# A tilted list schedule, z on VectorE alone, V shifted by DMA, and q and k in pieces

## The chip, the cores and the metric

One core of one Trainium2 chip. The metric is the device time of one execution in microseconds; less is better. Before: 210.66 us, the median of 3 runs (210.21 to 212.92). A profiled execution has a span (first to last instruction) some 2 us shorter than its time; the one of before took 208.38 us, 2.3 less than the median. On one core a run is called slow when it lies over 1.5% above the fastest run of the same kernel; fast runs are compared with fast runs. The kernel before was run beside every experiment on the same chip, and the ratios below are against those runs.

## The reference, cut to what matters

```python
# attention: 4 batches, 8 heads, 768 positions, 64 per head
scores = q @ k.T / 8                      # causal; heads 0, 2, 6 see all of it ("retrieval"),
                                          # heads 1, 3, 4, 5, 7 a window of 64 and 4 sink rows ("streaming")
x = softmax(scores) @ v                   # heads side by side: 768 x 512
# token mix
theta = x @ w_theta
y = w_tok_r @ (x * cos(theta)) + w_tok_i @ (x * sin(theta))   # "zr" and "zi"
u = x + y
out = u + relu(u @ w_ch)
```

## The kernel before, the parts that matter

The kernel is a list of steps, each with its possible engines and a duration. A list scheduler in the kernel's own program orders them by rank (the longest way to the end), and each engine then runs its steps in that fixed order. The order is static: on the chip an engine whose next step is not ready waits, even if later ones are.

```python
# a step may name two engines; the scheduler picks one
zs[b, "r", i + y] = add("DVE", 690, z_real, [c] + old, give=[c], port=True)
zs[b, "i", i + y] = add({"DVE": 690, "POOL": 1250}, 0, z_imag, [s] + old, give=[s], port=True)
...
cast[b, n] = add({"DVE": 570, "POOL": 830}, 0, cast_v, [land] + old, give=[issue], port=True)   # V to bf16
shift[b, h] = add({"DVE": 340, "POOL": 960}, 0, shift_v, [cast[b, n]] + old, port=True)         # V by 64 rows, streaming heads
...
def load_steps(b, after):                 # q and k of a batch: one transfer each, from GpSimd's queue
    for what in "qk":
        issue = add("POOL", 900, lambda: load_qk(what, b, slice(0, 8)), after + last_pool, bias=-20000)
        land = add("DMA", 5000, None, [issue])
...
first = add("SP", 1500, lambda: sink_values(2 * half), ...)     # sink rows of V for two batches
land = add("DMAH", 300, None, [first])
sink_done.append(add("DVE", 480, <cast of them into vs>, [land, ...]))
...
order = plan.order({"PE": 0, "ACT": 2100, "DVE": 2500, "POOL": 7500, "SP": 750})
for s in order:                           # emitted in the order of planned start
    ...
```

The softmax here doesn't subtract the row's maximum and nothing guards it: scores larger than these inputs give would overflow.

## Time and profile before

TensorE has 179.0 us of work in a span of 206.3. The prediction below cuts the span into windows and shows in which of them TensorE stands idle. In the profile's lines PE is TensorE and PEld its weight loads, DVE is VectorE, ACT ScalarE, POOL GpSimd and SP SyncE; a q behind the name (SPq) means the engine's queue. The two groups that carry z are shown here (line, engine, operation, shapes and count, then busy us, mean ns of one, then idle time before them and what ended it):

```profile
L243 POOL TENSOR_TENSOR zi<-x,st 128x512 bf16<-128x512 bf16 x11 | 14.7, 1350 | 29.0 <-ACT st L486 28.9
L243 DVE TENSOR_TENSOR zr<-x,ct 128x512 bf16<-128x512 bf16 x24 | 22.9, 992 | 1.5 <-ACT ct L484 1.5
```

GpSimd does 11 of the 24 zi; VectorE's zr take 992 ns in the mean beside them.

### The profile page before, as it was taken

To read this page: it belongs to the slowest core of one execution; us is meant where nothing else is said; L and a number is where in the kernel's file an instruction comes from. 1 tells how busy PE (TensorE), PEld (TensorE's weight loads), DVE (VectorE), ACT (ScalarE), POOL (GpSimd) and SP (SyncE) were. 2 spreads that over 40 slices of the span, in tenths; PEclk is the share of its full clock that TensorE was granted. 3 is DMA by queue.
4 is the path that set the end of the run, shared out by engine and by line. 5 is a ranking of instruction groups with operands and counts; after the bars stand their busy time and mean duration, and the time that the engine had idled before them with its cause. 6 is when DMAs were issued, how large, how long until landed. Compare 5 with 4: busy or idle time off the path is not lost.

```text
span 206.3 us, 4846 instructions
## 1 busy us (share of the span) xinstructions
PE 179.0 (87%) x1988; PEld 99.4 (48%) x1988; DVE 134.2 (65%) x236; ACT 108.7 (53%) x135; POOL 76.1 (37%) x140
## 2 busy tenths in 40 slices
PE   0689599667999999999999999989699999597992
PEld 0436388444546584454653557534335664242440
DVE  7336966389984574799855287499917446944442
ACT  2397914789885735550677464696683427300010
POOL 8966960394752000674123200099350002900000
PEclk9999999999999999999999999999999999999999
DMA  5998999999999995952223047784223254113404
GB/s 169 182 222 168 157 199 196 192 202 208 206 204 204 115 126 134 232 144 102 54 81 126 4 78 130 185 180 96 49 81 102 79 102 105 55 47 76 153 25 152
DMA packets 58252, 27.45 MB, mean 133 GB/s; under 512 B 44408, under 2 KB 55160, under 8 KB 58232
## 3 DMA queue, kind: packets, MB, share of 16 engines
q1 hardware_dynamic: 47704, 17.85, 40.6%
q0 software_dynamic: 10528, 9.31, 28.3%
q8 instruction: 15, 0.25, 0.6%
q14 instruction: 5, 0.04, 0.1%
HBM read 25.71 MB, written 6.29 MB: 155 GB/s over the span
## 4 chain that ended last, share of the span: by engine, by line
PE 64%; DVE 14%; DMA 13%; ACT 4%; POOL 2%; issue 1%; DVEq 0%; POOLq 0%
PE bank L502 28%; PE bank L525 9%; DMA qb<-in_q_dram 8%; PE pair L366 7%; DVE zr L243 7%; PE pair L453 7%; PE pair L479 6%; PE bank L300 5%; DMA kb<-in_k_dram 3%; DVE zi L243 2%; DVE qT L240 1%; DMA uT<-u 1%; DVE vx L240 1%; PE bank L545 1%; DMA out_dram<-ot 1%
## 5 line engine op out<-in xcount | busy, mean ns | idle before, releaser
L502 PE MATMUL bank<-zr,wtokTr 128*128 128x512 bf16 x144 | 38.6, 380 | 4.3 <-DVE zr L243 3.4
L502 PE MATMUL bank<-zi,wtokTi 128*128 128x512 bf16 x144 | 38.3, 379 | 0.2 <-DVE zi L243 0.2
L366 PE MATMUL pair<-qT,kT 64*64 64x128 bf16 (+5 forms) x380 | 26.7, 262 | 5.1 <-ACT P L385 2.1
L506 DVE TENSOR_TENSOR u<-x,bank 128x512 bf16<-128x512 bf16 x24 | 16.3, 684 | 18.6 <-PE bank L502 18.5
L525 PE MATMUL bank<-w_ch_sb,uT 128*128 128x512 bf16 x96 | 24.1, 380 | 1.9 <-DMA uT<-u 1.5
L247 POOL TENSOR_SCALAR_AFFINE_SELECT P<-P 128x256 bf16<-128x256 bf16 (+1 forms) x48 | 18.2, 398 | 20.1 <-ACT P L385 11.0
L243 POOL TENSOR_TENSOR zi<-x,st 128x512 bf16<-128x512 bf16 x11 | 14.7, 1350 | 29.0 <-ACT st L486 28.9
L529 DVE SCALAR_TENSOR_TENSOR ot<-bank,u 128x512 f32<-128x512 f32 x24 | 16.5, 689 | 13.5 <-PE bank L525 13.2
L243 DVE TENSOR_TENSOR zr<-x,ct 128x512 bf16<-128x512 bf16 x24 | 22.9, 992 | 1.5 <-ACT ct L484 1.5
L366 PEld LDWEIGHTS <-kT 64*64 64x64 bf16 (+1 forms) x380 | 13.0, 111 | 22.4 <-issue 19.5
L385 ACT ACTIVATE P<-pair 128x1024 bf16<-128x1024 f32 (+2 forms) x24 | 21.8, 922 | 3.0 <-PE pair L366 2.8
L479 PE MATMUL pair<-w_theta_sb,xT 128*128 128x512 bf16 x96 | 22.8, 379 | 0.3 <-ACT st L486 0.2
L502 PEld LDWEIGHTS <-wtokTi 128*128 128x128 bf16 x144 | 13.5, 98 | 17.3 <-issue 2.1
L502 PEld LDWEIGHTS <-wtokTr 128*128 128x128 bf16 x144 | 12.6, 98 | 18.9 <-issue 6.5
L382 ACT ACTIVATE P_st<-pair 128x512 bf16<-128x512 f32 (+1 forms) x16 | 12.8, 813 | 12.9 <-PE pair L366 12.8
L240 ACT COPY uT<-bank 128x512 bf16<-128x512 bf16 x5 | 2.9, 585 | 29.3 <-PE bank L515 29.3
L240 POOL CAST vt<-st_v 128x768 bf16<-128x768 f32 x9 | 10.3, 1167 | 20.7 <-DMA st_v<-in_v_dram 20.6
L484 ACT ACTIVATE ct<-pair,half_pi 128x1024 f32<-128x1024 f32 x12 | 13.1, 1118 | 8.0 <-PE pair L479 5.1
L460 DVE TENSOR_TENSOR x<-pair,r 128x512 bf16<-128x512 f32 x24 | 16.6, 691 | 0.8
L453 PE MATMUL pair<-vx,P_st 128*128 128x65 bf16 x120 | 16.0, 200 | 0.3 <-DVE P_st L402 0.3
L300 PE MATMUL bank<-ident,kb 128*64 128x128 bf16 x192 | 8.9, 244 | 8.4 <-DVE kb L240 5.2
L453 PE MATMUL pair<-vt,P_st 128*128 128x65 bf16 x120 | 16.0, 200 | 0.0
(77 smaller groups left out, 291.6 us busy)
## 6 DMA issues: line engine op xcount, KB each, us to landing
st_v<-in_v_dram SPq DMA_DIRECT2D x32, 192.0 KB
out_dram<-ot SPq DMA_DIRECT2D x24, 256.0 KB
qb<-in_q_dram POOLq DMA_DIRECT2D x3, 768.0 KB, 16.8
kb<-in_k_dram POOLq DMA_DIRECT2D x3, 768.0 KB, 19.6
wtok<-in_moe_w_tok_r_dram POOLq DMA_DIRECT2D x3, 384.0 KB, 15.4
wtok<-in_moe_w_tok_i_dram POOLq DMA_DIRECT2D x3, 384.0 KB, 16.6
w_theta_sb<-in_moe_w_theta_dram POOLq DMA_DIRECT2D x1, 512.0 KB, 9.5
w_ch_sb<-in_moe_w_ch_dram POOLq DMA_DIRECT2D x1, 512.0 KB, 24.3
```

The lines of the kernel that those rows point to most:

```text
L240: {"ACT": nc.scalar.copy, "DVE": nc.vector.tensor_copy, "POOL": nc.gpsimd.tensor_copy}[state["step"].eng](o, i)
L243: {"DVE": nc.vector, "POOL": nc.gpsimd}[state["step"].eng].tensor_tensor(o, a, b, ALU.mult)
L247: nc.gpsimd.affine_select(out=t, in_=t, compare_op=ALU.is_ge, fill=0.0, base=base, pattern=pattern, channel_multiplier=cm)
L300: nc.tensor.transpose(pt[64 * x:64 * x + 64, j * 128:(j + 1) * 128], state[what, b][:, h, j * D:(j + 1) * D], ident)
L366: nc.tensor.matmul(ps[half, yy, c:c + w], l, r, start=True, stop=True, skip_group_check=True)
L385: nc.scalar.activation(P.rearrange("p (y c) -> p y c", y=2), ps[:, :, :w0], AF.Exp, scale=scale)
L453: nc.tensor.matmul(o, l, r, start=(m == 0), stop=True, skip_group_check=True)
L460: nc.vector.tensor_tensor(dst, av[:, :, :, :D], r.unsqueeze(3).to_broadcast([128, 2, 4, D]), ALU.mult)
L479: nc.tensor.matmul(ps[:, y], state["xT", b][:, kk, (i + y) * 128:(i + y + 1) * 128], w_theta_sb[:, kk], start=(kk == 0), stop=(kk == KD - 1))
L502: nc.tensor.matmul(py, wtokT[n][:, s, t * 128:(t + 1) * 128], z[:, s], start=(g == 0 and m == 0), stop=(g == 2 and m == 3))
L525: nc.tensor.matmul(pc, uT[:, kk], w_ch_sb[:, kk], start=(kk == 0), stop=(kk == KD - 1))
L529: nc.vector.scalar_tensor_tensor(ot, state.pop(("pc", b, t)), 0.0, state.pop(("u", b, t)), ALU.max, ALU.add)
```

## The change

Its intent: a table of 800-odd numbers, found by a search against the schedule's own model of durations, is added to the ranks; some durations of that model are corrected; VectorE and GpSimd are no longer planned to work at the same time on operations that want their common port; all of z goes to VectorE; V of batches 1 to 3 is shifted by DMAs from SyncE (SP); q and k of batches 1 to 3 come two heads at a time, and those of batches 2 and 3 are held back until the token mix two batches earlier runs.

```diff
+TILT = [
+    -82, 155, -168, 19, 0, 0, 358, 0, 91, 190, 0, 406, 514, 399, -109, -295, 17, -173, 57, -465, -136, -201, -239,
+    ...                                    (cut: 42 more rows)
+]
+        self.tilt = {n: 100 * t for n, t in enumerate(TILT)}
...
+        for n, ns in self.tilt.items():
+            rank[n] += ns
...
+                other = {"DVE": "POOL", "POOL": "DVE"}.get(e)
+                busy = other and port[other] and free[other] > now
                 for s in ready[e]:
+                    if busy and s.port:
+                        continue
...
+    def move_v(b):
+        for s, h in ((slice(0, 1), slice(4, 5)), (slice(1, 5), slice(1, 8, 2))):
+            nc.sync.dma_start(out=vx[:64, s], in_=vt[:64, h])
+            nc.sync.dma_start(out=vx[64:, s, 1:], in_=vt[64:, h, :NB - 1])
...
-                if not IS_RETR[h]:
-                    shift[b, h] = add({"DVE": 340, "POOL": 960}, 0, ... shift_v ..., [cast[b, n]] + old, port=True)
+                if not IS_RETR[h] and b == 0:
+                    shift[b, h] = add({"DVE": 510, "POOL": 1000}, 0, ... shift_v ..., [cast[b, n]], port=True)
+        if b:
+            move = add("SP", 1400, lambda b=b: move_v(b), [cast[b, n] for n in (1, 2, 3)] + old)
+            moved = add("DMAH", 500, None, [move])
...
-                zs[b, "i", i + y] = add({"DVE": 690, "POOL": 1250}, 0, ... z_imag ..., [s] + old, give=[s], port=True)
+                zs[b, "i", i + y] = add("DVE", 690, ... z_imag ..., [s] + old, give=[s], port=True)
...
+            if t < 4 and b + 2 < B:
+                load_steps(b + 2, t, [kept[what, b, n] for what in "qk" for n in range(4)] + [mixed[b, t, 2]])
...
-    def load_steps(b, after):
+    def load_steps(b, n, after):
+        heads = slice(PAIRS[n][0], PAIRS[n][1] + 1, 2)
         for what in "qk":
-            issue = add("POOL", 900, ... load_qk(what, b, slice(0, 8)) ...)
+            issue = add("POOL", 750, ... load_qk(what, b, heads) ...)
-    load_steps(1, [])
+    for n in range(4):
+        load_steps(1, n, [])
(cut: durations, such as normalize 850 -> 920 and waves 930 -> 1000, one term of the rank formula, and helper lines)
```

## The prediction

> **What bounds the kernel now.** I read the page's busy times first, then the table of windows, the list of waits, and last the timeline of each stall, engine by engine. The busy times:
>
> ```profile
> span 206.3 us, 4846 instructions
> PE 179.0 (87%) x1988; PEld 99.4 (48%) x1988; DVE 134.2 (65%) x236; ACT 108.7 (53%) x135; POOL 76.1 (37%) x140
> ```
>
> TensorE is the bound: 179.0 of 206.3 us, so at most 27.3 us can be won by filling its holes. No part of the change removes a matmul. The windows (window: length, then busy time of PE, weight load, DVE, ACT, POOL, then clock, DMA share, GB/s) say where the holes are:
>
> ```profile
> 0.00:8.84 8.84, 1.65 (x24) 1.22 (x24) 5.07 (x12) 2.88 (x3) 7.55 (x18) 1.00 0.85 172
> 8.84:31.40 22.56, 18.82 (x257) 13.38 (x258) 14.36 (x32) 14.97 (x21) 16.25 (x39) 1.00 1.02 188
> 31.40:57.40 26.00, 20.51 (x312) 13.48 (x310) 20.34 (x36) 20.05 (x26) 13.50 (x20) 1.00 1.24 200
> 57.40:131.00 73.60, 73.60 (x845) 39.98 (x845) 48.50 (x89) 40.40 (x51) 17.89 (x36) 1.00 0.71 122
> 131.00:150.00 19.00, 16.36 (x173) 8.22 (x172) 17.55 (x25) 14.66 (x19) 12.19 (x17) 1.00 0.56 130
> 150.00:172.60 22.60, 22.60 (x267) 11.93 (x265) 10.14 (x21) 10.70 (x14) 2.88 (x8) 1.00 0.39 93
> 172.60:189.00 16.40, 12.41 (x57) 5.33 (x56) 11.67 (x14) 4.43 (x5) 5.87 (x4) 1.00 0.22 67
> 189.00:206.30 17.30, 13.02 (x66) 5.87 (x64) 6.55 (x10) 0.58 (x1) 0.00 (x0) 0.98 0.32 106
> ```
>
> The PE idles 7.2 us before the first data, 3.7 to 31.4 us, 5.5 to 57.4 us, nothing in the long middle, 2.6 at 131 to 150 us, 4.0 at 172.6 to 189 us, and 4.3 in the last window, the tail of last finishes and stores. Start and tail (11.5 us) are touched by nothing here. That leaves 15.8 us to be won.
>
> The second fact is the collision of DVE and POOL over z. In the timeline (start, length, engine, line, instruction, idle before) of the last batch's z:
>
> ```profile
> 173.39 0.68 DVE L243 TENSOR_TENSOR zr<-x,ct 128x512 bf16<-128x512 bf16 x1
> 174.59 4.43 DVE L243 TENSOR_TENSOR zr<-x,ct 128x512 bf16<-128x512 bf16 x3
> 174.17 5.87 POOL L243 TENSOR_TENSOR zi<-x,st 128x512 bf16<-128x512 bf16 x4 [19.71 <-ACT st L486]
> 179.07 2.53 PE L502 MATMUL bank<-zr,wtokTr 128*128 128x512 bf16 x11 [1.19 <-DVE zr L243]
> ```
>
> Three zr take 4.43 us beside POOL's zi, 1.48 each against 0.68 alone; the PE waits for them. The third is the start of batch 1, where all of q and k comes in one transfer each:
>
> ```profile
> 41.36 0.86 PE L300 MATMUL bank<-ident,qb 128*64 128x128 bf16 x24 [1.71 <-DMA qb<-in_q_dram]
> 43.01 0.86 PE L300 MATMUL bank<-ident,qb 128*64 128x128 bf16 x24 [0.79 <-DVE qT L240]
> 46.82 1.20 PE L300 MATMUL bank<-ident,kb 128*64 128x128 bf16 x36 [0.89 <-DMA kb<-in_k_dram]
> 50.11 1.02 PE L502 MATMUL bank<-zr,wtokTr 128*128 128x512 bf16 x4 [0.86 <-DVE kT L240]
> ```
>
> **What the Trainium skill says.** "SBUF — State Buffer", section "SBUF: two separate sides": the port pair that VectorE and GpSimd share is an exclusive lock for a whole instruction, taken also by a VectorE operation with two SBUF inputs against a GpSimd operation that reads SBUF. The trace agrees: zr has a median of 688 ns, a mean of 992 and a maximum of 2168. "DMA: Bandwidth & Descriptors", section "SWDGE vs HWDGE vs iDMA": transfers issued from SyncE do not use GpSimd's descriptor path, so the shift of V cannot be locked out by VectorE. The same page, section "Anatomy of one DMA", puts some 2 us of fixed cost on each transfer of the GpSimd path. Nothing in this trace isolates that: the large q and k loads took 16 to 20 us under a saturated DMA. "TensorE: Matmul & The Clock Gate", Part 1: the array runs at half rate until it has been busy for some 3.4 us. The trace agrees in kind: 24 transposes took 1.49 us at 16.8 us and 0.86 at 41.4, and the fast pace begins only at 31.4 us, though the page's clock row shows full clock throughout.
>
> **The change part by part.**
>
> z on VectorE. 11 products of 1350 ns leave POOL (14.7 us). They add 11 x 0.68 = 7.5 us to DVE, but the stretch goes: zr 22.9 - 24 x 0.69 = 6.3 and zi 11.9 - 13 x 0.69 = 2.9. So DVE is no busier (-1.7), and throughput gains nothing. In the last batch, from 173.39, twelve products and three finishes at the 0.60 us start-to-start of undisturbed ones are 9.0 us, to 182.4; with POOL's help the last one ended at 182.39, the same. What changes is the order: the first mixing group wants four zr only. Alone on DVE they can be ready at 173.4 + 4 x 0.60 = 175.8, or 177.0 behind two finishes, against 179.0. The PE waited 1.30 + 1.19 = 2.5 us there; I take 2.0. Likewise 0.7 at 137 to 139 us, and 0.8 of the wait for kT at 50 us, a copy that stood on DVE behind three stretched zr (4.02 us). Sum 3.5.
>
> q and k in pieces. For batch 1 only the first pair of heads has to land before its transposes, a quarter of each transfer. The waits at 41 to 47 us are 1.71 + 0.79 + 0.89 = 3.4 us. The DMA stays saturated (share 1.24) so the bytes needed come no sooner in sum; I take 2.5. Batches 2 and 3 used to load at 41.8 to 53 us, into that saturated stretch; now they wait for the token mix, where the DMA share is 0.7 or less. This relieves the token weights and costs nothing as long as they land before about 98 and 122 us. POOL issues grow from 6 to 24, 18 x 0.75 = 13.5 us, about what z gives back.
>
> V shifted by DMA. 15 of 20 streaming heads lose two copies of some 0.25 us each: 7.6 us of mostly DVE work. One block of it (2.62 us at 142.4) stands before the u additions, but PE's next wait is for exponentials, not for these. SP gets 12 transfers of some 0.4 to 0.5 us each. V was cast by 146 and is first multiplied at 156, so a landing some us later hides. On the path: 0.3.
>
> The tilted priorities. They aim at what is left of the 15.8: 1.7 at 146 to 150 (PE waits for exponentials that it fed too late), 1.5 at 186.8 (a wait for the transpose of u), and 3.7 before 31.4. That is 6.9; being a static order tuned for a model of durations, I give it 40%, 2.7. The chain also has 24 groups of four large matmuls that take 0.97 instead of 0.86 us because they alternate with the score matmuls' tile shape; this 2.6 us may shrink or grow by some 1 us and is not counted.
>
> Sum: 3.5 + 2.5 + 0.3 + 2.7 = 9.0 us of gain. Off that I take 1.5 for new collisions: POOL issues before causal masks, SP blocked on a V shift ahead of the transposes of x, and order that the chip does not follow as modelled. Net 7.5: 210.7 - 7.5 = 203.2.
>
> **The rivals.** (a) VectorE becomes the bound around each theta stage. For it: DVE is busy 17.55 of 19.0 us at 131 to 150, and all 12 products of a batch are now its own. Against it: without the stretch and the V shift its total falls to about 134.2 - 1.7 - 7.6 = 125 us. It would leave the z gain at zero or below: 207 us. (b) The gain is all in the schedule and larger: PE has 15.8 us of holes, and if an earlier dense start makes the array fast before 31.4 us, some of the 18.8 busy us before it halve. Against it: to 57 us the DMA is saturated, so earlier speed mostly buys more waiting. It would make 198 us. (c) The tilt was tuned on wrong durations and the waits only move: late q and k pieces behind the mix they are gated on, or the SP queue blocked. The profile can neither exclude nor show it; the middle has no slack, so any new hole there adds in full: 208 to 211 us.
>
> **Range and chances.** (a), (b) and (c) span 198 to 211; eight times in ten I expect 198.5 to 208.5, about my sum with a gain from a quarter of it to a third more. Faster by over 2% needs under 206.4, a net gain of 4.3 us, less than half of the holes' 15.8: 0.75. Within 2%: 0.22. Slower: 0.03, since nothing adds TensorE work.
>
> **What would show it.** Right: PE still about 179 us busy with a span near 199; no product on POOL; zr with mean close to its median of 0.69; PE's wait for zr under 1 us in total instead of 3.4; the transposes of batch 1 starting before 41 us with less than 1 us of waits for q and k; POOL about 70 us busy, DVE about 125. Wrong: PE waits on DVE in the theta stages as long as before (rival a), PE busy well under 175 us because the fast pace begins earlier (rival b), or new waits for pieces of q and k, or for V, in the middle (rival c).

## The result, and the profile after

After: 203.17 us, the median of 4 runs (202.94 to 205.1), against 210.81 (210.21 to 212.92) of before on the same chip. The ratio is 0.964, 95% interval 0.955 to 0.973. Ratios here are the mean time of one kernel's fast runs over that of the other's in the same rounds, so not quite the ratio of the medians quoted. The total is the predicted 203.2. The rest of this document asks whether it came about as predicted, and in its parts mostly it did not. The same kernel measured again on another chip (e8 below) came to 0.978.

The page of the profile after, its span and busy times:

```profile
span 201.1 us, 4814 instructions
...
PE 178.0 (88%) x1961; PEld 99.1 (49%) x1988; DVE 128.2 (64%) x229; ACT 104.6 (52%) x129; POOL 67.8 (34%) x141
```

27 of the 1988 matmul records are missing (the weight loads are complete), so PE's 178.0 is a little low. DVE and POOL stand near where the prediction put them (about 125 and about 70). The windows of after, cut at the same places as before (window: length, busy time of PE, weight load, DVE, ACT, POOL, then clock, DMA share, GB/s):

```profile
8.84:31.40 22.56, 18.19 (x279) 13.19 (x278) 14.84 (x33) 15.32 (x22) 16.73 (x41) 0.92 1.07 197
31.40:57.40 26.00, 21.40 (x267) 12.59 (x272) 17.29 (x29) 16.09 (x19) 11.97 (x20) 0.87 1.09 181
57.40:131.00 73.60, 71.38 (x844) 39.80 (x857) 48.35 (x86) 41.97 (x53) 21.67 (x45) 1.00 0.83 135
131.00:150.00 19.00, 18.74 (x182) 8.46 (x185) 13.53 (x20) 15.12 (x19) 8.51 (x16) 1.00 0.77 159
172.60:189.00 16.40, 16.35 (x76) 7.45 (x76) 10.64 (x17) 2.16 (x3) 0.00 (x0) 1.00 0.33 88
```

From 172.6 to 189 PE is busy 16.35 of 16.40 us, where it was busy 12.41: the hole at the last batch's z is gone. But from 31.4 to 57.4 us it still idles 4.6 us, and there the granted clock falls to 0.87. The timeline of that stall (start, length, engine, line, instruction; in brackets the idle time before it and what ended it), with SP's queue under it:

```profile
49.15 0.56 DVE L288 CAST vt<-st_v 128x768 bf16<-128x768 f32 x1 [3.66 <-DMA st_v<-in_v_dram]
49.63 0.95 DVE L288 COPY kT<-bank 128x768 bf16<-128x768 bf16 x1
57.20 0.49 DVE L824 CAST vs<-vs_f 96x640 bf16<-96x640 f32 x1 [2.50 <-DMA vs_f<-in_v_dram]
50.63 1.44 PE L598 MATMUL bank<-ident,wtok 128*128 128x128 bf16 x12 [3.96 <-DVE kT L288]
52.44 1.89 PE L555 MATMUL bank<-zi,wtokTi 128*128 128x512 bf16 x4
49.78 0.65 SPq L334 DMA_DIRECT2D vx<-vt  x1
51.13 1.97 SPq L346 DMA_DIRECT2D vs_f<-in_v_dram  x5
```

VectorE stands 3.66 us at the cast of a piece of V that has not landed, though the copy of kT behind it could go. PE waits 3.96 us for that copy. After this idle time it runs cold, at about half its pace: four mixing matmuls take 1.89 us where four take 1.03 elsewhere in the same trace (granted clock 0.50 from 50 to 54 us). Then VectorE stands again, 2.50 us, at the cast of the sink rows of V (vs): their load stands on SP behind the V shift, which waits for that same cast of V.

To see where time is won or lost I counted the weight loads that each kind of matmul had issued by a given time, and weighted them with the pace on the chain: 0.216 us for a 512-wide one (four in 0.86), 0.030 for one of the values, 0.033 for a transpose of q or k (24 in 0.79), 0.0555 for one of a token weight (12 in 0.67), and 0.058 for a score (an estimate of mine for their mixed widths). All together make 160.1 us of work. Work done by each time, in us:

```
time        45     50     60     90     131    150    172.6  189
before     20.8   23.2   31.8   60.0   99.2  115.1  136.4  148.3
after      23.3   24.8   31.7   58.8   97.7  115.0  137.5  153.9
e1 no tilt 23.3   27.7   34.9   63.3  102.3  117.7  139.4  152.2
e3 z POOL  23.0   27.3   33.2   59.8   95.7  112.7  135.1  151.1
e7 mended  24.3   28.2   38.2   64.0  102.4  119.1  142.2  158.4
```

After is 2.5 us ahead at 45, has lost it by 60, is behind at 131, level at 150, and wins 4.5 us between 172.6 and 189. In the profiled runs all of the gain is made in the last quarter.

### The profile page after: what moved, and what is told of

It reads as the page before. It is cut to its first block, busy times and chain, and to the rows that moved or that the text cites. A ratio compares the mean times of both kernels' runs of the same rounds, so it can differ in the third digit from the quotient of the medians.

```text
span 201.1 us, 4814 instructions
## 1 busy us (share of the span) xinstructions
PE 178.0 (88%) x1961; PEld 99.1 (49%) x1988; DVE 128.2 (64%) x229; ACT 104.6 (52%) x129; POOL 67.8 (34%) x141
## 4 chain that ended last, share of the span: by engine, by line
PE 71%; DMA 15%; ACT 5%; DVE 5%; issue 2%; SPq 0%; DVEq 0%; ACTq 0%
PE bank L555 28%; DMA st_v<-in_v_dram 10%; PE bank L578 9%; PE pair L419 9%; PE pair L532 8%; PE pair L506 8%; PE bank L353 6%; DMA xT<-x 3%; DMA uT<-u 3%; PE bank L598 2%; DVE zi L291 1%; ACT P_st L435 1%; PE bank L568 1%; ACT P L438 1%; DVE P_st L629 1%
## 5 line engine op out<-in xcount | busy, mean ns | idle before, releaser
L555 PE MATMUL bank<-zi,wtokTi 128*128 128x512 bf16 x139 | 39.0, 391 | 0.6 <-issue 0.5
L555 PE MATMUL bank<-zr,wtokTr 128*128 128x512 bf16 x134 | 37.2, 380 | 0.7 <-issue 0.2
L419 PE MATMUL pair<-qT,kT 64*64 64x128 bf16 (+6 forms) x380 | 26.2, 258 | 4.0 <-ACT P L438 1.5
L578 PE MATMUL bank<-w_ch_sb,uT 128*128 128x512 bf16 x89 | 23.3, 380 | 1.2 <-ACT uT L288 0.7
L291 DVE TENSOR_TENSOR zr<-x,ct 128x512 bf16<-128x512 bf16 x24 | 17.5, 760 | 3.4 <-ACT ct L537 3.0
L291 DVE TENSOR_TENSOR zi<-x,st 128x512 bf16<-128x512 bf16 x24 | 17.7, 758 | 0.0
L455 DVE TENSOR_TENSOR P_st<-P_st,m_stream 128x512 bf16<-128x512 bf16 (+2 forms) x24 | 12.0, 507 | 6.3 <-ACT P_st L435 5.2
L506 PE MATMUL pair<-vx,P_st 128*128 128x65 bf16 x120 | 15.5, 198 | 0.0
L506 PE MATMUL pair<-vt,P_st 128*128 128x65 bf16 x120 | 15.5, 198 | 0.0
L506 PE MATMUL pair<-vt,P 128*128 128x65 bf16 x252 | 14.9, 199 | 0.5 <-ACT P_st L435 0.5
```

The costliest lines, as they stand in the source:

```text
L291: {"DVE": nc.vector, "POOL": nc.gpsimd}[state["step"].eng].tensor_tensor(o, a, b, ALU.mult)
L419: nc.tensor.matmul(ps[half, yy, c:c + w], l, r, start=True, stop=True, skip_group_check=True)
L506: nc.tensor.matmul(o, l, r, start=(m == 0), stop=True, skip_group_check=True)
L555: nc.tensor.matmul(py, wtokT[n][:, s, t * 128:(t + 1) * 128], z[:, s], start=(g == 0 and m == 0), stop=(g == 2 and m == 3))
L578: nc.tensor.matmul(pc, uT[:, kk], w_ch_sb[:, kk], start=(kk == 0), stop=(kk == KD - 1))
```

## The experiments

Twelve runs, on three chips; e7 repeats e4, and e8 repeats after. "Order unchanged" means that the finished order was kept and only the named instructions were moved or given to another engine; without that, every small edit would have the schedule made anew.

| run | based on | edit | ratio to before (95%) | median us |
|---|---|---|---|---|
| after, first chip | | | 0.964 (0.955 to 0.973) | 203.17 |
| e8, after again | after | none | 0.978 (0.969 to 0.986) | 205.90 |
| e1 | after | tilt emptied | 0.976 (0.966 to 0.985) | 204.66 |
| e2 | before | zi to VectorE, order unchanged | 0.990 (0.978 to 1.001) | 208.51 |
| e3 | after | 11 zi to GpSimd, order unchanged | 0.996 (0.984 to 1.007) | 209.80 |
| e4, e7 | after | V cast and V shift of batch 1 later | 0.949, 0.950 (0.944 to 0.955) | 197.93, 198.49 |
| e5 | e4 | V shift on VectorE | 0.956 (0.950 to 0.963) | 199.91 |
| e6 | e4 | q, k of batch 1 whole | 0.989 (0.981 to 0.997) | 206.77 |
| e9 | after | sink load ahead of V shift only | none (see below) | 202.66 |
| e12 | e4 | sink load again behind V shift | 0.984 (0.976 to 0.993) | 206.96 |
| e10 | before | q, k of batch 1 in pieces | 1.009 (1.001 to 1.018) | 211.07 |
| e11 | before | z, pieces and V by DMA at once | 0.990 (0.981 to 0.998) | 206.50 |

All gave correct results. e1 to e4 ran on one chip (before: median 208.38), e5 to e8 on a second (209.49), e9 to e12 on a third (209.15).

**e1: the change without the tilt.**

```diff
-        self.tilt = {n: 100 * t for n, t in enumerate(TILT)}
+        self.tilt = {}
```

> The kernel after with the tilt table emptied; everything else of the change is kept (z on VectorE, V shifted by DMA, q and k in pieces, the new durations of the model). If my sum of the prediction holds part by part, the parts other than the tilt keep some 6.3 us less their 1.5 us of collisions, so about 206 us. Rival: the gain is all in the order, and the other parts pay nothing by themselves: 209 to 212 us.

Ratio 0.976, near the expected 206 (which is 0.977 of before's 210.8). The parts other than the tilt do carry 2.4% when the order is made anew for them. The tilt adds 1.2% by after's first measurement and nothing by its second (0.978), so between these two kernels it is not shown to pay. The table of work says why: e1 has no stall at 46 to 50 us and is 3.2 us ahead of after at 60; the tilt wins it back at the end. Windows of e1:

```profile
131.00:150.00 19.00, 17.55 (x126) 7.34 (x125) 12.62 (x22) 13.75 (x17) 4.60 (x12) 0.91 0.59 120
172.60:189.00 16.40, 13.07 (x61) 5.69 (x60) 9.24 (x16) 2.21 (x3) 0.00 (x0) 1.00 0.21 58
```

In the last of them PE idles 3.3 us, nearly as before (4.0); in after 0.05. In before the hole is two waits, 2.5 us for zr and 1.5 for the transpose of u; in e1 they are 1.86 and 1.47. Between e1 and after, closing it is the tilt's work: after has the first theta of the last batch start at 164.2 us, between the last value matmuls, and keeps mixing matmuls of the batch before for the wait; the kernel before starts it at 167.4. The schedule's own estimates for its orders (its planned end, from running the kernels' planner off the chip) were 194.6 us for before, 195.3 for e1 and 184.7 for after; on the chip the spans were 206.3, 202.8 and 201.1. Of the 10.6 us that the search won in its model, 1.7 showed.

**e2 and e3: z on VectorE or GpSimd, each in the other kernel's order.**

```diff
+    for key, s in zs.items():                       # e2, in the kernel before, after the order is made
+        if key[1] == "i":
+            s.eng = "DVE"
+    for b, t in ((0, 2), (0, 0), (1, 0), ...):      # e3, in after: the 11 that before had there
+        zs[b, "i", t].eng = "POOL"
```

> The kernel before with its 11 zi products of GpSimd given to VectorE at the same places of the same order; nothing else moves. Theory of the prediction: PE's waits for zr (3.4 us) nearly go, zr falls to about 0.7 us mean, and the time falls by 2 to 3.5 us, to 207 to 209. Rival: VectorE becomes the bound in the theta stages, since its total work there is the same: within 0.5 us of 210.8.

> The kernel after with the same 11 zi products put back on GpSimd, order unchanged; the converse of the run before. Theory: the collisions return, zr's mean goes to 0.9 to 1.0 us, and 2 to 3.5 us are lost: 205.5 to 207. Rival (order alone): the tilted order computes theta earlier, so z has slack, and the time stays within 0.7 us of 203.2.

In before's order the move is worth 1.05% (2.2 us), though the interval just includes nothing and only two of e2's four runs count as fast. The mechanism is plain in its groups:

```profile
L243 DVE TENSOR_TENSOR zi<-x,st 128x512 bf16<-128x512 bf16 x24 | 17.7, 773 | 0.0
L243 DVE TENSOR_TENSOR zr<-x,ct 128x512 bf16<-128x512 bf16 x24 | 16.0, 696 | 1.5 <-ACT ct L484 1.5
```

zr falls from 992 to 696 ns, and PE's waits for zr fall from 3.4 us to 1.0. At the last batch's z, where before waits 2.5 us, this is left:

```profile
174.74 2.53 PE L502 MATMUL bank<-zr,wtokTr 128*128 128x512 bf16 x11 [0.72 <-DVE zr L243]
```

So in before's order z alone wins 1.8 of the 2.0 us that the prediction put down for this place, with no tilt. DVE is no busier (132.7 us against 134.2), as worked out, so the profile speaks against the rival of VectorE as the new bound; the times alone do not exclude it.

In after's order, giving 11 products back loses more: 0.996 against 0.964 or 0.978, so 1.8 to 3.2% (3.7 to 6.6 us). These runs are from different chips, and the interval overlaps that of the 0.978. The timeline of e3:

```profile
96.67 4.23 DVE L291 TENSOR_TENSOR zi<-x,st 128x512 bf16<-128x512 bf16 x1 [1.03 <-ACT st L539]
96.32 2.27 POOL L291 TENSOR_TENSOR zi<-x,st 128x512 bf16<-128x512 bf16 x2
98.55 0.82 POOL L288 CAST vt<-st_v 128x768 bf16<-128x768 f32 x1
99.33 1.03 POOL L295 TENSOR_SCALAR_AFFINE_SELECT P<-P 128x128 bf16<-128x128 bf16 x4
```

One product of 0.68 us takes 4.23: it waits through two products, a cast and four masks that GpSimd runs back to back. A tighter order has less slack to hide that. Something like it is left in after, from GpSimd's casts of V alone: two zr of 1.81 and 1.26 us and one zi of 2.21 us, each beside such a cast. It is why z's mean there is 0.76 and not the 0.69 that I expected.

**e4 and e7, e8: the cast of V out of the head of VectorE's queue.**

```diff
     order = plan.order(...)
+    late = [cast[1, 3], moves[1]]            # moves[b] is the V shift's issue
+    order = [s for s in order if s not in late]
+    at = order.index(zs[0, "r", 5]) + 1      # seven VectorE instructions later
+    order[at:at] = late
```

> The kernel after, but VectorE's cast of the last piece of batch 1's V (and the V shift behind it) put five VectorE instructions later than the plan has it. In the trace after, VectorE stands 3.66 us at that cast until V lands at 49.15 us; the copy of kT behind it holds TensorE for 3.96 us, after which TensorE runs at half clock until 56 us. Theory: the head of the line is the cause, TensorE's wait goes under 1.5 us and the time falls by 2 to 5 us, to 198 to 201. Rival: the stage is bound by the DMA anyway (share over 1.2 until 55 us), the wait only moves to the next transfer: 202.5 to 204.

> The kernel of e4 (after with one V cast and one V shift later), once more, beside after itself on the same chip. Theory (the cast at the head of VectorE's queue costs a stall of 4 us and the cold clock behind it): 2 to 5 us under after of this batch. Rival: the difference of e4 to after was that of two chips: within 1 us of after.

> The kernel after unchanged, as the yardstick of this batch: 0.955 to 0.973 of before. Its stall in batch 1 hangs on when one transfer of V lands (49.15 us in its profile, 45.5 in that of e3, which has the same order up to there), so its runs should scatter more than those of e7.

The expectation says five instructions; in the order, and in the traces of e4 and e7, it is seven. The mended kernel runs at 0.949 and, on another chip, at 0.950 of before. After beside it on that second chip is at 0.978, so the two moved steps are worth 2.9% (0.978 / 0.950), some 5.8 us. Windows of e7, and its cast of the sink rows, now without a wait:

```profile
31.40:57.40 26.00, 25.44 (x307) 13.78 (x304) 21.41 (x36) 20.31 (x25) 13.04 (x23) 1.00 1.14 190
172.60:189.00 16.40, 16.40 (x80) 7.54 (x79) 7.77 (x12) 0.00 (x0) 0.00 (x0) 1.00 0.33 96
50.12 0.48 DVE L827 CAST vs<-vs_f 96x640 bf16<-96x640 f32 x1
```

PE is busy 25.44 of the 26.0 us where it was busy 21.40, at full clock and with the DMA as loaded as ever. So the rival (the DMA bounds this stage) falls. Against e1, on one chip, the mended kernel is 2.7% better (0.949 / 0.976): that is what the tilt is worth once the stalls are gone, which e1's trace does not have.

e8's ratio, 0.978, lies outside the 0.955 to 0.973 that I expected, and my reason for its scatter held only in part. In its profile V had landed in time (the cast at 45.26 us did not wait), and yet VectorE then stood 4.63 us at the cast of the sink rows, and PE 3.52 us. That run counts as slow and lost time elsewhere too (between 60 and 90 us it did 22.3 us of work where after did 27.1), but e3, whose profiled run is fast and keeps after's order, shows the same:

```profile
45.47 0.55 DVE L288 CAST vt<-st_v 128x768 bf16<-128x768 f32 x1
55.76 0.49 DVE L824 CAST vs<-vs_f 96x640 bf16<-96x640 f32 x1 [3.97 <-DMA vs_f<-in_v_dram]
```

Moving the V shift had mended two things at once.

**e9 and e12: the two halves of the mend.**

```diff
+    order = [s for s in order if s is not moves[1]]          # e9, in after: only SP's order is changed
+    order.insert(order.index(<sink load's issue>) + 1, moves[1])
-    late = [cast[1, 3], moves[1]]                            # e12, in e4: VectorE's order of e4, SP's of after
+    late = [cast[1, 3], moves[1], <sink load's issue>]
```

> The kernel after with only this moved: SyncE issues the load of the sink rows of V for batches 2 and 3 ahead of batch 1's V shift instead of behind it; VectorE's order, with the V cast at the head, stays. e4 had moved both. In after, VectorE also stood 2.5 to 4.6 us at the cast of those sink rows. If the V cast is the cause of after's loss: the ratio stays that of after, 0.964 to 0.978. If the sink load behind the V shift is: the 0.95 of e4.

> The other half of e4: the V cast later on VectorE, but the sink rows' load again behind the V shift on SyncE. If the V cast is the cause: 0.95. If the sink load is: 0.964 to 0.978. If each stall alone lets the other take its place: both halves stay above 0.96.

e12 (only the V cast later) gives 0.984: no gain over after, and not the 0.95 expected if the V cast were the cause. The stall has moved behind the next head of the queue:

```profile
57.64 0.49 DVE L827 CAST vs<-vs_f 96x640 bf16<-96x640 f32 x1 [6.54 <-DMA vs_f<-in_v_dram]
59.25 0.61 PE L568 MATMUL bank<-ident,u 128*128 128x128 bf16 x4 [5.29 <-DVE u L559]
52.05 2.28 SPq L346 DMA_DIRECT2D vs_f<-in_v_dram  x5
```

e9 (only the sink load ahead of the V shift) scatters: 196.38, 199.50 and 200.79 in three runs, 204.54 to 205.71 in the other three. No ratio is given, since only the first counts as fast. The one with a profile (200.79) had V landed in time, its cast starting at 45.78 without a wait. That the three long runs are those in which V came late is a guess, since they have no trace. So my theory of the V cast was at most half the cause. The sink load behind the V shift is shown: it made VectorE stand 2.5 to 6.5 us in every trace that has it (after, e3, e8, e12), and with VectorE's order kept it makes the difference between 0.949 (e4) and 0.984 (e12; another chip, but the intervals lie far apart). Of the four traces with the V cast at the head (after, e3, e8, e9) it stalled in after's alone, where V landed late; that both must be mended rests on e9's scatter and is not shown.

**e5: the V shift back on VectorE.**

```diff
-            nc.sync.dma_start(out=vx[:64, s], in_=vt[:64, h])          # and the second half alike
+            for s1, h1 in zip(range(5)[s], range(8)[h]):
+                nc.vector.tensor_copy(vx[:64, s1], vt[:64, h1])        # ten copies a batch
```

> The kernel of e4 with V of batches 1 to 3 shifted by VectorE copies, ten for a batch, at the place where the DMA was issued. Prediction: the V shift is worth 0.3 us on the path, so at most 1 us over e7. Rival: the 2.6 us of copies for each batch stand ahead of the copies of q and k and of the mixing's additions, now that VectorE does all of z: 2 to 4 us over e7.

0.956 against 0.950, 1.4 us in the medians, where at most 1 was expected; the intervals overlap, so it is likely and not shown. VectorE is 8.2 us busier (136.3 against 128.1), and most of it hides. The shift's own gain is small, though the 0.3 us of the prediction looks low; what it did to SP's queue cost several times as much.

**e6 and e10: q and k of batch 1 whole, or in pieces.**

```diff
-    load_qk(what, b, heads)                                                            # e6, in e4
+    load_qk(what, b, heads) if b > 1 else load_qk(what, b, slice(0, 8)) if n == 0 else None
-    load_qk(what, b, slice(0, 8))                                                      # e10, in before
+    for heads in (four slices if b == 1 else [slice(0, 8)]): load_qk(what, b, heads)
```

> The kernel of e4 with q and k of batch 1 fetched whole again, one transfer each at the places of the first pieces. Prediction: pieces are worth 2.5 us in batch 1, so 1.5 to 3.5 us over e7. Rival: the DMA is saturated and what the PE lacks is the sum of bytes, so within 0.8 us of e7.

> The kernel before with q and k of batch 1 fetched in four pieces each (q first, then k) at the places of the whole loads; order otherwise unchanged. The waits of TensorE on those loads are 2.6 us in its profile. Prediction's value of pieces: 1.5 to 2.5 us gained, ratio 0.988 to 0.993. Theory after e6 (there pieces were worth 8 us because the order asks for them early): before's order asks for all of q before k, so little, 0.99 to 1.0.

Undone in the mended kernel, the pieces are worth 4.1% (0.989 / 0.950), about 8.2 us, where I had expected 1.5 to 3.5. The trace of e6 shows why:

```profile
38.82 0.85 PE L353 MATMUL bank<-ident,qb 128*64 128x128 bf16 x12 [2.17 <-DMA qb<-in_q_dram]
44.20 0.53 PE L353 MATMUL bank<-ident,kb 128*64 128x128 bf16 x12 [1.81 <-DMA kb<-in_k_dram]
```

PE waits 4.0 us for the whole transfers, but by 60 us it has done 30.5 us of work where e7 has done 38.2. The granted clock is 0.81, 0.76 and 0.67 in the stretches 36 to 40, 40 to 44 and 44 to 48 us, where e7 has 1.00: twelve transposes took 0.85 us after the first wait and 0.53 once the pace was full. So here the loss is about twice the waits; that the slow pace is the rest of it rests on this one trace. Done in the kernel before, they lose 0.9% (interval 0.1 to 1.8). The same transfers, so it is the order that makes them pay: the mended order asks for q and k of single pairs between theta and mixing matmuls from 36 us on, the kernel before for all of q and then all of k. And pieces cost something that I had not counted. GpSimd's issues in e10:

```profile
29.23 0.72 POOL L255 DMA_DIRECT2D kb<-in_k_dram  x1 [0.99 <-DMA wtok<-in_moe_w_tok_r_dram]
32.31 0.71 POOL L255 DMA_DIRECT2D kb<-in_k_dram  x1 [2.36 <-DMA wtok<-in_moe_w_tok_i_dram]
33.41 0.71 POOL L542 DMA_DIRECT2D wtok<-in_moe_w_tok_r_dram  x1 [0.39 <-DMA qb<-in_q_dram]
```

GpSimd waits for the landing of the transfer eight issues back before it issues another. It is a wait of the program: in the packed trace each issue from the ninth on waits for the semaphore that the issue eight before it raises on landing, and eight of them (103 to 110) go round. So with eight pieces the next token weights are issued at 33.41 us instead of 27.35. Whether this alone is the 0.9% is open; PE's wait for q (1.71 us) did go, and one of 2.52 us for a copy of kT came.

**e11: three parts in the order of before.**

> The kernel before, order unchanged, with three parts of the change at once: z on VectorE, batch 1's q and k in pieces, V of batches 1 to 3 shifted by DMA. My sum for these parts was 6.3 us less collisions: ratio 0.970 to 0.985. Rival: the parts gain only where the order is made anew for them (as in e1, 0.976), so here the 0.99 of z alone.

0.990 (0.970 to 0.985 was expected), the same as z alone. The edit joins e2's and e10's and puts the four DMAs of the V shift at the place of the last shift of each batch. Without a new order, pieces and V shift gain nothing more: the rival held.

## Why the prediction was right, and where it was not

The time was 203.17 for a predicted 203.2, and the direction was shown; the sum came out right with terms that were not. That it fits to the last digit is luck: by the second measurement, 0.978, it would be 206.0 us. Step by step:

- **z on VectorE, 3.5 us.** Mechanism right. 2.2 us in before's order (interval just touching nothing), 3.7 to 6.6 in after's. PE's waits for zr went from 3.4 us to 1.0 by the move alone (e2) and to 0.2 (for a weight load) in after, and DVE got no busier, so rival (a) did not show. But in e1's order 2.6 us of them remain, so the order has its share. Not foreseen: GpSimd's casts of V still stretch three products, to 1.26, 1.81 and 2.21 us.
- **q and k in pieces, 2.5 us.** The step was mis-sized both ways. By themselves they lose 1.9 us; in the order made for them they are worth 8.2. I had argued from the lengths of the waits at 41 to 47 us alone, one of which (0.79) was for a copy on VectorE and not for a transfer; the slow clock that waits leave behind (0.67 to 0.81 in e6) was not in the sum. Those waits went (PE waits for no q or k in after's profile, and batch 1's transposes start at 36.5 us instead of 41.4), but 3.96 us of another wait took their place in the profiled run.
- **V shifted by DMA, 0.3 us.** Small for itself, as said (1.4 us in e5, not clear of noise). But SP's queue is where the largest single loss of the change came from.
- **The tilt, 2.7 us.** Right in kind: of the three holes that I aimed it at, two are closed in after and open in e1 (1.25 + 0.20 us of waits for exponentials near 143 us, 1.47 for the transpose of u). The third, before 31.4 us, is not its work: e1 has done the same 23.3 us of work by 45 us. Beside that it closes the 1.86 us that e1 keeps of the wait for zr of the last batch, a place that I had put down to z. Its measured worth is 0 to 1.2% (0 to 2.5 us) as the change stands and 2.7% (5.5 us) with the two stalls mended.
- **Collisions, minus 1.5 us.** The kind was right (I had named SP blocked on a V shift), the victim wrong (the sink rows' load, not the transposes of x), and the size too small: 5.8 us with the cast of V. Rival (c), waits that only move, was thus true of the first third of the run, and one of its signs, a new wait for V, came true. Rival (b) did not show: PE is busy 178.0 us, not well under 175.

So the errors of size cancelled in part. The mended kernel gains some 10.5 us (0.950 of 210.7), where my terms of gain came to 9.0. The two stalls take 5.8 of that by the second measurement of after, or 3.0 by the first, where I had allowed 1.5. The single worths above add up to more than these 10.5 us, so they overlap.

The better version is the mended one: 0.950 of before and 2.9% under after, with the same TensorE order.

## What to carry to other kernels

In a static order an instruction that waits for a transfer holds everything behind it on its engine; put it behind whatever is ready, above all where the DMA is saturated and landing times are uncertain (one transfer of V landed by 45.3 in one run and at 49.15 us in another of the same kernel). A transfer that depends on compute does the same to its DMA queue: independent loads belong ahead of it. Do not add up the worth of parts measured singly: pieces were worth minus 1.9 us in one order and plus 8.2 in another, so try each part both alone and taken out of the whole. And do not price a wait of TensorE by its length alone: look at the pace of the matmuls after it.

## What the Trainium skill lacked or had wrong

- "SBUF — State Buffer", "SBUF: two separate sides", says that the loser of the shared port blocks for the whole instruction. The runs show that it can be longer: one VectorE product of 0.68 us took 4.23 us, through a row of seven GpSimd instructions. The page does not say who comes next when GpSimd has more work ready.
- No page says that issues from GpSimd's queue wait for one another. In these programs each issue from the ninth on waits for the landing of the one eight before it, on a semaphore that both use (up to 2.36 us, in e10). It is the program's own wait; no limit of the chip is shown.
- "DMA: Bandwidth & Descriptors", "Anatomy of one DMA", has some 2 us of fixed cost on GpSimd's path and gives no landing time for a transfer among many others. In after the pieces of 192 KB took a median of 6.0 to 6.5 us to land, and SyncE's V shifts 6.7 to 8.7 us from SBUF to SBUF, so landing times for a schedule must come from a trace.
